# Query tails in 512-byte packets with quarter products, and other places for the choice products, three weight loads and the layout of the final choice

## The chip, the cores and the metric

The kernel runs on one core of one Trainium2 chip. The metric is the device time of one execution in microseconds (us), as the median over several runs. A core has five engines, each with its own in-order instruction stream: TensorE (PE, with its weight loads PEld), VectorE (DVE), ScalarE (ACT), GpSimd (POOL) and SyncE (SP). Here SP mostly issues transfers, and 16 DMA engines carry them out.

## The reference

Three layers, one behind the other. The first is a linear attention over 8 batches, 8 heads, 576 rows and a head width of 64; its output is normed per row and head. The rows then go through a mixture of 8 experts with one choice per row, and its output through a second mixture in which every expert takes exactly 576 rows.

```python
kv = np.einsum('bhsd,bhse->bhde', k, v)
out = np.einsum('bhsd,bhde->bhse', q, kv)
rms = np.sqrt(np.mean(out * out, axis=-1, keepdims=True) + 1e-06)
attn = out / rms * g_norm
...
logits = xn @ en.T / tau
expert_idx = np.argmax(logits, axis=1)
...
out[mask] = gate_w[mask, None] * (np.maximum(x[mask] @ w1[e], 0.0) @ w2[e])
...
flat = (x @ w_gate).flatten()
for idx in np.argsort(-flat):
    tok, e = int(idx) // E, int(idx) % E
    if assigned[tok] >= 0 or counts[e] >= cap:
        continue
    assigned[tok] = e
```

## The kernel before

**Attention.** The 8 batches go in 4 groups of 2 (`gi` 0 to 3). `kv(b)` multiplies k and v of a batch (line L295) and turns the result with the gate weights (L312). The queries go in 10 steps a group (`UNITS`): 8 steps of 4 heads by 256 rows, and 2 steps (`u == 4`) for the last 64 rows of each batch, the tail. `qa` transposes a step's queries on PE (L336) and copies them out on ACT (L337, `qT`); `qb` multiplies them with kv (L353, for the tail L359), and ACT and DVE carry the result out of PSUM (L368 or L370, L373, L375). `qa` runs two steps ahead of `qb`. The queries of 512 rows a batch come in by `load_main`, the tails by `load_tail`, where each packet is one row of one head, 64 floats or 256 bytes.

**Choice of the first expert.** When a group is done, `group_end` runs as a generator beside the next group's steps, a piece at each step: norms, the argmax, then `slots`, which counts the rows of each expert with two small matmuls against `trm` and `ones` (L477, L478, the "choice products"), and places each row by a matmul of one-hot rows (L517) into `table`. `WAITS` says how many steps `slots` holds back before the choice products and before L517. For the last group the generator runs beside the first expert's matmuls; `PEW` says how many us of those matmuls (after a plan of columns / 2400 us) PE issues between its pieces.

**First expert, early.** During the last group the first 320 rows of expert 0 are gathered; they are multiplied with their norms on DVE (`normed`, L654), transposed into tiles (`xtile`, L694), and split into a high half (ACT, L697) and a low half (DVE, L698). `XT0` names the step of each of the 3 tiles, its first entry also the step of the norms. Then `first0` streams layer 1 (L739, L740, L742) and `layer2_apart` (L810, L811, L808) through PE. Each weight is loaded raw (`wload`, on SP), cast on ACT (L567) and its low half taken on DVE (L573, partly put off into `LSUB`); three raw buffers go round. The remaining rows of expert 0 are gathered as soon as `tabi` (L1004) is there.

**Final choice.** After 8 rounds of bounds (`da_round`), `da_choice` writes the chosen expert of each row into `Pf` (L1193), and `table2` counts (L1250, L1251), scans (L1254) and places the rows (L1286). Matmuls of the last experts fill PE between the pieces.

In every engine the order is the order in which the program text calls; there is no scheduler.

## Time and profile before

| | |
|---|---|
| median of 3 runs | 1037.05 us (1033.49 to 1037.54) |
| profiled execution | 1037.28 us, of which the span of its instructions 1035.4 us |
| PE busy | 999.9 us, 97% of the span |
| DVE, ACT, POOL busy | 70%, 51%, 18% |
| DMA, 10 to 110 us | 16 engines busy throughout, 276 to 385 GB/s in stretches of 10 us |
| PE clock, mean | 0.995 of full |

The time is that of one execution from outside; the span runs from the first to the last instruction in the trace. The timeline gives for each row its start, its length, and in brackets how long the engine was idle before it and what ended that. A group of rows has one length for all of them. Matmuls in float32 are counted twice in these views (x16 for 8 instructions).

### The profile page before, as it was taken

The numbers are of one execution on the slowest core, as the hardware profiler recorded it, in microseconds if no ns is written. First come the engines' busy times: TensorE is split into PE (matmuls) and PEld (weight loads), VectorE is DVE, ScalarE is ACT, GpSimd is POOL, SyncE is SP. The second block draws the span as 40 slices with busy tenths as digits, with TensorE's granted clock in tenths as the row PEclk, the third lists the DMA queues.
The fourth block names the chain that finished last, engine by engine and source line by source line (L and its number), as shares of the span: only waits on it lengthen the run. The fifth ranks groups of instructions, "written<-read, shape, count | busy, mean of one in ns | idle before, by whom it ended". The sixth has DMA issues, their size and how long they took to land. (4 is left out here: it accounts for less than half of the span.)

```text
span 1035.4 us, 20479 instructions
## 1 busy us (share of the span) xinstructions
PE 999.9 (97%) x8177; PEld 920.5 (89%) x8177; DVE 729.5 (70%) x1513; ACT 528.0 (51%) x913; POOL 181.6 (18%) x310
## 2 busy tenths in 40 slices
PE   7888899999999999999999999999999999999998
PEld 6777799999999999999988889898989898989896
DVE  4466877569878878786876774859495858676760
ACT  2566836664545354444542323656555555656551
POOL 2000123101010201011001113131313132222211
PEclk9999999999999999999999999999999999999999
DMA  9999666544434344332402025342434242525211
GB/s 286 368 338 350 199 222 213 163 163 141 147 99 160 110 141 130 128 128 90 152 1 83 22 73 205 130 154 103 154 102 154 102 158 100 172 94 162 102 47 46
DMA packets 94679, 152.46 MB, mean 147 GB/s; under 512 B 11321, under 2 KB 52281, under 8 KB 94579
## 3 DMA queue, kind: packets, MB, share of 16 engines
q1 hardware_dynamic: 85539, 122.18, 35.4%
q0 software_dynamic: 9040, 28.93, 8.8%
q8 instruction: 65, 1.06, 0.4%
q14 instruction: 35, 0.29, 0.1%
HBM read 121.26 MB, written 29.82 MB: 146 GB/s over the span
## 5 line engine op out<-in xcount | busy, mean ns | idle before, releaser
L739 PE MATMUL mm<-xh,whi 128*128 128x256 f32 (+7 forms) x512 | 153.7, 300 | 0.9 <-ACT xh L697 0.5
L740 PE MATMUL mm<-xl,whi 128*128 128x256 f32 (+7 forms) x512 | 151.0, 295 | 0.3 <-issue 0.3
L742 PE MATMUL mm<-xh,wlo 128*128 128x256 f32 (+7 forms) x512 | 150.0, 295 | 0.0
L779 PE MATMUL mm<-hh,whi 128*128 128x256 f32 (+7 forms) x480 | 146.0, 304 | 0.0
L780 PE MATMUL mm<-hl,whi 128*128 128x256 f32 (+7 forms) x480 | 142.4, 297 | 0.0
L781 PE MATMUL mm<-hh,wlo 128*128 128x256 f32 (+7 forms) x480 | 142.1, 296 | 0.0
L573 DVE TENSOR_TENSOR wlo<-wraw,whi 128x1024 fp32r<-128x1024 f32 x71 | 86.5, 1223 | 32.1 <-ACT whi L567 31.0
L739 PEld LDWEIGHTS mm<-xh,whi 128*128 128x128 f32 x512 | 96.3, 188 | 2.4 <-ACT xh L697 0.7
L740 PEld LDWEIGHTS mm<-xl,whi 128*128 128x128 f32 x512 | 96.3, 188 | 0.5 <-issue 0.5
L742 PEld LDWEIGHTS mm<-xh,wlo 128*128 128x128 f32 x512 | 96.0, 188 | 0.0
L913 DVE SCALAR_TENSOR_TENSOR rc<-xg,big 128x512 bf16<-128x512 f32 x128 | 88.2, 689 | 8.6 <-ACT big L905 5.6
L779 PEld LDWEIGHTS mm<-hh,whi 128*128 128x128 f32 x480 | 91.3, 190 | 1.5 <-issue 0.5
L780 PEld LDWEIGHTS mm<-hl,whi 128*128 128x128 f32 x480 | 91.3, 190 | 0.0
L781 PEld LDWEIGHTS mm<-hh,wlo 128*128 128x128 f32 x480 | 90.8, 189 | 0.0
L791 ACT COPY yT<-mm 128x512 f32<-128x512 f32 (+7 forms) x29 | 18.5, 638 | 138.2 <-PE mm L781 138.2
L672 POOL DMA_INDIRECT xg<-xbuf,tabi x40 | 43.3, 1084 | 194.1 <-ACT sj L619 90.9
L567 ACT CAST whi<-wraw 128x1024 fp32r<-128x1024 f32 x71 | 73.9, 1043 | 1.2 <-DMA wraw<-in_moe_w 1.1
L748 ACT ACTIVATE hh<-mm 128x512 fp32r<-128x512 f32 (+7 forms) x56 | 36.8, 657 | 66.7 <-PE mm L742 66.0
L1943 DVE TENSOR_TENSOR wlo<-wraw,whi 128x1024 fp32r<-128x1024 f32 (+1 forms) x63 | 61.0, 988 | 11.6 <-ACT whi L1946 11.6
L2200 POOL DMA_INDIRECT out<-tm,ti x38 | 41.4, 1089 | 145.8 <-ACT tm L2198 126.3
L749 DVE SCALAR_TENSOR_TENSOR hl<-mm,hh 128x512 fp32r<-128x512 f32 (+7 forms) x56 | 42.7, 762 | 27.5 <-ACT hh L748 26.0
L2185 PE MATMUL mA<-whi,hx 128*128 128x512 f32 x136 | 56.9, 418 | 0.0
(402 smaller groups left out, 2607.7 us busy)
## 6 DMA issues: line engine op xcount, KB each, us to landing
wraw<-in_moe_w SPq DMA_DIRECT2D x127, 512.0 KB
kmain<-in_k SPq DMA_DIRECT2D x16, 576.0 KB
vmain<-in_v SPq DMA_DIRECT2D x16, 576.0 KB
xbuf<-xo SPq DMA_DIRECT2D x16, 528.0 KB
qmain<-in_q SPq DMA_DIRECT2D x16, 512.0 KB
ybuf<-yr SPq DMA_DIRECT2D x29, 260.0 KB
xg<-in_moe_w SPq DMA_DIRECT2D x16, 256.0 KB
xg<-in_moe_w_gate SPq DMA_DIRECT2D x8, 256.0 KB
```

What stands on the lines that cost most here:

```text
L567: nc.scalar.copy(hi, raw)
L573: eng.tensor_tensor(lo, raw, hi.bitcast(F32), op=OP.subtract)
L672: nc.gpsimd.indirect_dma_start(out=xg[:n, :wd], out_offset=None, in_=buf[:, :], in_offset=bass.IndirectOffsetOnAxis(ap=idx[:n, e * SC + t: ...
L739: nc.tensor.matmul(o, a, xh[:, kd, :N], start=(kd == 0), stop=False)
L740: nc.tensor.matmul(o, a, xl[:, kd, :N], start=False, stop=False)
L742: nc.tensor.matmul(o, b, xh[:, kd, :N], start=False, stop=(kd == KD - 1))
L779: nc.tensor.matmul(o, a, hh[:, kf, :N], start=(kf == 0), stop=False)
L780: nc.tensor.matmul(o, a, hl[:, kf, :N], start=False, stop=False)
L781: nc.tensor.matmul(o, b, hh[:, kf, :N], start=False, stop=(kf == KF - 1))
L913: V.scalar_tensor_tensor(junk, raws[i], 1.0, wgB[:, x], op0=OP.mult, op1=OP.mult, accum_out=w2g[:, i // KF, i % KF, x:x + 1])
L1943: V.tensor_tensor(l, x, h.bitcast(F32), op=OP.subtract)
L2185: nc.tensor.matmul(ps[:, x_, :], hh, a, start=(kf == 0), stop=False)
```

## The change

- `load_tail` brings the tail in packets of 2 rows of one head (512 bytes), in 4 transfers instead of 2 a group; partition 64 j + 32 hh + p holds rows 2p and 2p+1 of batch j for the heads of half hh.
- `qa` turns the whole tail at once (4 transposes and one copy of 512 columns, instead of twice 2 transposes and a copy of 256); `qb` forms the tail's products in quarters, 16 matmuls of 64 x 32 weights instead of 8 of 64 x 64 a step. Stores of the tail's rows and the row numbers (`tokf`) follow the new order, in 4 transfers instead of 2.
- The norms of expert 0's first tiles stay at step 5 (`NORM0`), the tiles move from steps 5, 6, 6 to 6, 6, 7. `WAITS` is per group: for group 2 the choice products go one step later, and L517 stays at its step.
- `PEW` changes, so that the last group's choice products and L517 are issued earlier between the first expert's matmuls. The low half of layer 1's last piece goes to `LSUB`, behind `table`, `tabi` and two low halves of weights.
- Three weight loads (8 to 10) leave `first0`'s put-off pieces on SP and are issued from ACT, one behind each of the tiles 3 to 5.
- `Pf` is stored by expert and then column, the order in which the matmuls and the sums of `table2` read it.

```diff
-PEW = (3.3, 6.2, 0.0, 0.4, 5.3)
+PEW = (3.3, 4.2, 2.0, 0.4, 4.1)
...
-XT0 = (5, 6, 6)
+NORM0 = 5
+
+XT0 = (6, 6, 7)
...
-WAITS = (1, 3)
+WAITS = ((1, 3), (1, 3), (2, 2), (0, 1))
...
-        t = mk(ap, [128, H, D], F32, nm + "tail", bufs=1)
+        t = mk(ap, [128, 4, 2, D], F32, "qtail", bufs=1)
         for j in range(2):
-            nc.sync.dma_start(t[64 * j:64 * j + 64], src(s, ((2 * gi + j) * H * S + 512) * D,
-                                                        [[D, 64], [S * D, H], [1, D]]))
+            for hh in range(2):
+                p = 64 * j + 32 * hh
+                nc.sync.dma_start(t[p:p + 32].rearrange("p h r d -> p h (r d)"),
+                                  src(q, ((2 * gi + j) * H * S + 4 * hh * S + 512) * D, [[2 * D, 32], [S * D, 4], [1, 2 * D]]))
...
+        if (u, hg) == (4, 1):
+            QT[gi, u, hg] = QT[gi, u, 0]
+            return
...
-            for h in range(2):
-                for s in range(2):
-                    for jj in range(2):
-                        nc.tensor.matmul(ov[64 * jj:64 * jj + 64, s, h],
-                                         qT[64 * s:64 * s + 64, h, 64 * jj:64 * jj + 64],
-                                         kvh(2 * gi + jj, 4 * hg + 2 * h + s)[64 * s:64 * s + 64, s], start=True, stop=True)
+            for h in range(4):
+                for jj in range(2):
+                    for r in range(2):
+                        p, c = 64 * jj + 32 * r, 64 * jj + 32 * hg
+                        nc.tensor.matmul(ov[p:p + 32, h % 2, h // 2], qT[64 * r:64 * r + 64, h, c:c + 32],
+                                         kvh(2 * gi + jj, 4 * hg + h)[64 * r:64 * r + 64, r], start=True, stop=True,
+                                         tile_position=(64 * r, p))
...
                 for j in range(2):
-                    b = 2 * gi + j
-                    nc.sync.dma_start(xbuf[b * S + 512:(b + 1) * S, :], x[64 * j:64 * j + 64, 0, :])
+                    for r in range(2):
+                        b, p = 2 * gi + j, 64 * j + 32 * r
+                        nc.sync.dma_start(xbuf[b * S + 512:(b + 1) * S, :].rearrange("(p r) d -> p r d", r=2)[:, r, :],
+                                          x[p:p + 32, 0, :])
...
+        def low(eng):
+            eng.scalar_tensor_tensor(hl, ps[:, :, :N], 0.0, hh.bitcast(F32), op0=OP.max, op1=OP.subtract)
+        if apart:
+            LSUB.append(low)
+        else:
+            low(V)
...
-            wcast(2 if f > 2 else 1, later=LSUB, ahead=3 if f else 4)
+            wcast(2 if f > 2 else 1, later=LSUB, ahead=4, load=(f == 0))
...
         xtiles(0, 0, 3 + i, 4 + i)
+        wload(RING + 1 + i, nc.scalar)
...
-    Pf = mk(mp, [128, NCOL, E], BF, "Pf")
+    Pf = mk(mp, [128, E, NCOL], BF, "Pf")
...
-        V.tensor_tensor(Pf, lm, m[:, :, None].to_broadcast([128, NCOL, E]), op=OP.is_ge)
+        V.tensor_tensor(Pf.rearrange("p e c -> p c e"), lm, m[:, :, None].to_broadcast([128, NCOL, E]), op=OP.is_ge)
...
-        Pe = Pf.rearrange("p c e -> p e c")
+        Pe = Pf
```

The order of PE's instructions around the first tail (group 0), before. `qtail` is the loaded tail, `kvx` the finished kv, `qT` the transposed queries; L359 are the tail's products, of which 2 of 8 are shown.

```order
L295 MATMUL mm<-kmain_87,vmain_88 64x64 x36
L336 MATMUL tp<-ident,qtail 128x128 x2
L353 MATMUL mm<-kvx_175,qT 128x144 x4
L312 MATMUL mm<-gex,kvn 128x72 x8
L336 MATMUL tp<-ident,qtail 128x128 x2
L353 MATMUL mm<-kvx_175,qT 128x144 x4
L295 MATMUL mm<-kmain_89,vmain_90 64x64 x36
L336 MATMUL tp<-ident,qmain 128x128 x4
L359 MATMUL mm<-kvx_174,qT 64x72
L359 MATMUL mm<-kvx_175,qT 64x72
```

The same place in the changed kernel, whose lines stand 3 to 16 further on (the products are L365, and 4 of 16 are shown).

```order
L298 MATMUL mm<-kmain_87,vmain_88 64x64 x36
L341 MATMUL tp<-ident,qtail 128x128 x4
L358 MATMUL mm<-kvx_177,qT 128x144 x4
L315 MATMUL mm<-gex,kvn 128x72 x8
L358 MATMUL mm<-kvx_177,qT 128x144 x4
L298 MATMUL mm<-kmain_89,vmain_90 64x64 x36
L341 MATMUL tp<-ident,qmain 128x128 x4
L365 MATMUL mm<-kvx_176,qT 32x72 x2
L365 MATMUL mm<-kvx_177,qT 32x72 x2
```

The four transposes stand together one step earlier, and each tail step has twice as many products of half the width.

The order on DVE in the last group, at steps 4 to 6, before. `s` are row sums of squares, `run` to `ue` the slot counts of group 2, `xg` and `kvx` the gathered rows of expert 0 under their norms (L654), `xl` the low half of their first tile (L698).

```order
L378 TENSOR_REDUCE s_1781<-sq 128x8 x2
L473 TENSOR_SCALAR run<-run 128x1
L482 SCALAR_TENSOR_TENSOR bs<-seg,sm 128x72
L484 TENSOR_TENSOR ue<-sm,run 128x72
L485 TENSOR_TENSOR ue<-ue,bs 128x72
L486 TENSOR_TENSOR run<-run,bs 128x8
L654 TENSOR_TENSOR xg_1822<-xg_1822 128x512
L654 TENSOR_TENSOR xg_1824<-xg_1824 128x512
L654 TENSOR_TENSOR kvx_174<-kvx_174 64x512
L378 TENSOR_REDUCE s_1781<-sq 128x8
L698 SCALAR_TENSOR_TENSOR xl_1962<-sm,gcol,xh_1961 128x4x128
L488 TENSOR_TENSOR ue<-ue,P 128x72
```

And in the changed kernel.

```order
L384 TENSOR_REDUCE s_1840<-sq 128x8 x2
L662 TENSOR_TENSOR xg_1881<-xg_1881 128x512
L662 TENSOR_TENSOR xg_1883<-xg_1883 128x512
L662 TENSOR_TENSOR kvx_176<-kvx_176 64x512
L384 TENSOR_REDUCE s_1840<-sq 128x8
L481 TENSOR_SCALAR run<-run 128x1
L490 SCALAR_TENSOR_TENSOR bs<-seg,sm 128x72
L492 TENSOR_TENSOR ue<-sm,run 128x72
L493 TENSOR_TENSOR ue<-ue,bs 128x72
L494 TENSOR_TENSOR run<-run,bs 128x8
L384 TENSOR_REDUCE s_1840<-sq 128x8
L706 SCALAR_TENSOR_TENSOR xl_2039<-sm,gcol,xh_2038 128x4x128 x2
```

The norms now stand ahead of the slot counts, and two tiles' low halves stand together behind them; the third tile's low half stands behind the ranks (`ue` to `sf`) as its second and third did.

The order on PE in `first0`, around the last group's choice products, before: L739 to L742 are layer 1's products in threes, and the rows behind L478 begin its last piece, in which they come in twos.

```order
L739 MATMUL mm<-xh_1961,whi 128x320
L740 MATMUL mm<-xl_1962,whi 128x320
L742 MATMUL mm<-xh_1961,wlo 128x320
L477 LDWEIGHTS trm
L477 MATMUL sm<-P,trm 128x72
L478 LDWEIGHTS ones
L478 MATMUL sm<-P,ones 128x72
L739 MATMUL mm<-xh_1961,whi 128x320
L740 MATMUL mm<-xl_1962,whi 128x320
L739 MATMUL mm<-xh_1961,whi 128x320
```

And in the changed kernel.

```order
L747 MATMUL mm<-xh_2038,whi 128x320
L748 MATMUL mm<-xl_2039,whi 128x320
L750 MATMUL mm<-xh_2038,wlo 128x320
L485 LDWEIGHTS trm
L485 MATMUL sm<-P,trm 128x72
L486 LDWEIGHTS ones
L486 MATMUL sm<-P,ones 128x72
L747 MATMUL mm<-xh_2038,whi 128x320
L748 MATMUL mm<-xl_2039,whi 128x320
L750 MATMUL mm<-xh_2038,wlo 128x320
```

The choice products now stand five threes earlier; L517 (not shown) stands five pairs of L810 and L811 earlier.

## Rows read from the trace of the kernel before

**Rows 1.** Head of the profile page.

```profile
span 1035.4 us, 20479 instructions
```

**Rows 2.** Stretches: us, busy PE, PEld, DVE, ACT, POOL; PE clock, DMA share, GB/s.

```profile
12.00:22.00 10.00, 7.37 (x192) 6.61 (x193) 4.79 (x21) 3.46 (x8) 0.00 (x0) 1.00 1.08 365
23.00:28.00 5.00, 3.35 (x88) 2.82 (x86) 1.38 (x2) 1.66 (x4) 0.00 (x0) 1.00 1.14 214
```

**Rows 3.** PE timeline: the longest wait for a load.

```profile
33.08 1.28 PE L295 MATMUL mm<-kmain,vmain 64*64 64x64 f32 x72 [2.28 <-DMA vmain<-in_v]
```

**Rows 4.** Transfers by line: the tails, with KB of one transfer.

```profile
qtail<-in_q SPq DMA_DIRECT2D x8, 128.0 KB
```

**Rows 5.** SP timeline: first tail load, and the weight loads 7 to 10.

```profile
16.97 3.29 SPq L142 DMA_DIRECT2D qtail<-in_q  x2
...
138.61 11.20 SPq L551 DMA_DIRECT2D wraw<-in_moe_w  x4
```

**Rows 6.** PE timeline: tail products, and rows beside them.

```profile
41.41 1.15 PE L353 MATMUL mm<-kvx,qT 128*128 128x144 f32 x8
...
47.86 0.48 PE L359 MATMUL mm<-kvx,qT 64*64 64x72 f32 x16
...
69.60 1.28 PE L295 MATMUL mm<-kmain,vmain 64*64 64x64 f32 x72
...
75.67 1.98 PE L312 MATMUL mm<-gex,kvn 64*128 64x72 f32 x16 [0.43 <-ACT lp L375]
...
82.70 1.28 PE L295 MATMUL mm<-kmain,vmain 64*64 64x64 f32 x72
...
103.70 1.11 PE L312 MATMUL mm<-gex,kvn 64*128 64x72 f32 x16 [1.71 <-ACT lp L375]
...
108.05 0.66 PE L336 MATMUL tp<-ident,qmain 128*128 128x128 f32 x4
```

**Rows 7.** DVE timeline: end of the last group, and its slot counts.

```profile
117.31 0.14 DVE L473 TENSOR_SCALAR run<-run 128x1 f32<-128x1 f32 x1
...
118.05 1.29 DVE L654 TENSOR_TENSOR xg<-xg 128x512 f32<-128x512 f32 x2
...
119.26 0.68 DVE L654 TENSOR_TENSOR kvx<-kvx 64x512 f32<-64x512 f32 x1
...
123.11 1.13 DVE L698 SCALAR_TENSOR_TENSOR xl<-sm,gcol,xh 128x512 fp32r<-128x512 f32 x2
...
136.63 0.30 DVE L482 TENSOR_TENSOR_SCAN bs<-seg,sm 128x72 f32<-128x72 f32 x1 [1.95 <-PE sm L478]
```

**Rows 8.** ACT timeline: wait for the counts, and third tile of the late rows.

```profile
117.49 0.20 ACT L474 COPY run<-run 128x8 f32<-128x8 f32 x1 [0.68 <-DVE run L473]
...
157.29 0.58 ACT L697 ACTIVATE xh<-tp,gcol 128x384 fp32r<-128x384 f32 x1 [1.66 <-PE tp L694]
```

**Rows 9.** PE timeline: first expert.

```profile
125.23 0.31 PE L740 MATMUL mm<-xl,whi 128*128 128x320 f32 x1
...
125.67 0.31 PE L740 MATMUL mm<-xl,whi 128*128 128x320 f32 x1
...
140.86 0.39 PE L810 MATMUL mm<-hh,whi 128*128 128x320 f32 x1 [0.75 <-DVE hl L749]
```

**Rows 10.** PE timeline: products of the final choice.

```profile
598.16 0.72 PE L1250 MATMUL mm<-Pf,ones 128*128 128x320 bf16 x1 [0.45 <-DVE Pf L1193]
...
599.38 0.30 PE L1252 MATMUL mm<-sl,ones 1*128 1x320 bf16 x1
```

**Rows 11.** DVE timeline: scan and masking of the final choice.

```profile
599.72 0.82 DVE L1254 TENSOR_TENSOR_SCAN rA<-seg,mm 128x320 f32<-128x320 f32 x1 [0.31 <-PE mm L1252]
...
601.36 0.74 DVE L1260 TENSOR_TENSOR rA<-rA,Pf 128x320 f32<-128x320 f32 x1
```

**Rows 12.** Two stretches, columns as in rows 2.

```profile
75.50:82.00 6.50, 6.33 (x48) 5.73 (x49) 1.76 (x3) 3.69 (x12) 0.00 (x0) 0.51 1.05 402
557.00:560.00 3.00, 3.00 (x17) 2.88 (x16) 2.48 (x7) 0.00 (x0) 0.87 (x1) 0.50 0.53 173
```

More of the change, by code (lines that the diff above doesn't have):

```diff
@@ L136, in fused_kernel, with load_tail @@
     LD = {}
-    def load_tail(gi, nm):
-        s = {"k": k, "v": v, "q": q}[nm]
-        t = mk(ap, [128, H, D], F32, nm + "tail", bufs=1)
+    def load_tail(gi):
+        t = mk(ap, [128, 4, 2, D], F32, "qtail", bufs=1)
         for j in range(2):
-            nc.sync.dma_start(t[64 * j:64 * j + 64], src(s, ((2 * gi + j) * H * S + 512) * D,
-                                                        [[D, 64], [S * D, H], [1, D]]))
-        LD[nm, "t", gi] = t
+            for hh in range(2):
+                p = 64 * j + 32 * hh
+                nc.sync.dma_start(t[p:p + 32].rearrange("p h r d -> p h (r d)"),
+                                  src(q, ((2 * gi + j) * H * S + 4 * hh * S + 512) * D, [[2 * D, 32], [S * D, 4], [1, 2 * D]]))
+        LD["q", "t", gi] = t
     def load_main(b, nm, hg):
@@ L222, in fused_kernel @@
     load_main(1, "q", 1)
-    load_tail(0, "q")
+    load_tail(0)
     load_kv(4)
@@ L329, in qa @@
         qT = mk(ap, [128, 4, 128], F32, "qT", bufs=3)
-        n = 4 if u < 4 else 2
-        for h in range(n):
+        for h in range(4):
             if u < 4:
@@ L334, in qa @@
             else:
-                a = LD["q", "t", gi][:, 4 * hg + 2 * h:4 * hg + 2 * h + 2, :]
+                a = LD["q", "t", gi][:, h]
             nc.tensor.transpose(pq[:, h, :], a.rearrange("p r d -> p (r d)"), ident)
-        nc.scalar.copy(qT[:, :n], pq[:, :n])
+        nc.scalar.copy(qT, pq)
         QT[gi, u, hg] = qT
@@ L346, in qb @@
         j, rr = divmod(u, 2)
-        qT = QT.pop((gi, u, hg))
+        qT = QT[gi, u, hg]
         po = mk(psum, [128, 2, 512], F32, "mm")
@@ L355, in qb @@
             ov = po[:, :, :2 * KW].rearrange("p a (c w) -> p a c w", w=KW)
-            for h in range(2):
-                for s in range(2):
-                    for jj in range(2):
-                        nc.tensor.matmul(ov[64 * jj:64 * jj + 64, s, h],
-                                         qT[64 * s:64 * s + 64, h, 64 * jj:64 * jj + 64],
-                                         kvh(2 * gi + jj, 4 * hg + 2 * h + s)[64 * s:64 * s + 64, s], start=True, stop=True)
+            for h in range(4):
+                for jj in range(2):
[4 more added lines that the diff above has]
+                                         tile_position=(64 * r, p))
         o3 = po[:, :, :n // 2 * KW].rearrange("p a (c w) -> p a c w", w=KW)
@@ L467, in slots @@
         def slots():
-            for i in range(0 if last else WAITS[0]):
+            for i in range(WAITS[gi][0]):
                 yield
@@ L512, in slots @@
                     [128, TG, NCOL // 2, 2]), op=OP.mult)
-            for i in range(1 if last else WAITS[1]):
+            for i in range(WAITS[gi][1]):
                 yield
@@ L570, in wcast, with rest @@
             up = WS["cast"] + ahead
-            def rest(eng, lo=lo, raw=raw, hi=hi, up=up):
+            def rest(eng, lo=lo, raw=raw, hi=hi, up=up, load=load):
                 eng.tensor_tensor(lo, raw, hi.bitcast(F32), op=OP.subtract)
@@ L706, in xtile @@
                 gate_in(e, t, p + n, xg)
-    GQ = []
+    GQ, LSUB = [], []
     def gates_in():
@@ L748, in layer1_g @@
         nc.scalar.activation(hh, ps[:, :, :N], AF.Relu)
-        V.scalar_tensor_tensor(hl, ps[:, :, :N], 0.0, hh.bitcast(F32), op0=OP.max, op1=OP.subtract)
+        def low(eng):
[4 more added lines that the diff above has]
+            low(V)
     tk = con([128, 2], I32, "tk")
@@ L970, in fused_kernel @@
         for j in range(2):
-            nc.gpsimd.iota(tokf[64 * j:64 * j + 64, gi, 8:9], pattern=[[0, 1]], base=(b0 + j) * S + 512,
-                           channel_multiplier=1, allow_small_or_imprecise_dtypes=True)
+            for r in range(2):
+                p = 64 * j + 32 * r
+                nc.gpsimd.iota(tokf[p:p + 32, gi, 8:9], pattern=[[0, 1]], base=(b0 + j) * S + 512 + r,
+                               channel_multiplier=2, allow_small_or_imprecise_dtypes=True)
     def split64(o, i, n):
@@ L1019, in fused_kernel @@
         if i == 9 and gi + 1 < NG:
-            load_tail(gi + 1, "q")
-        if gi == NG - 1 and i == XT0[0]:
+            load_tail(gi + 1)
+        if gi == NG - 1 and i == NORM0:
             for t in range(3):
@@ L1052, in fused_kernel @@
     MP[True] = mo0.enter_context(tc.tile_pool(name="moe0", bufs=1))
-    LSUB = []
     wload(RING - 1)
@@ L1685, in one_by_one @@
             V.tensor_tensor(Mv, Mv, ec[:, None, :].to_broadcast([128, NCOL, E]), op=OP.add)
-        V.tensor_copy(Pf.rearrange("p c e -> p (c e)"), A)
+        V.tensor_copy(Pf.rearrange("p e c -> p c e"), A.rearrange("p (c e) -> p c e", e=E))
         table2()
```

## The prediction, made before the change was run

> **What bounds the kernel now.** I read the head of the page first: the span is 1035.4 us [rows 1] and the profiled execution took 1037.28, so 1.9 us lie outside the span. The sum below is made against 1037.28; the median of the three runs, 1037.05, is 0.2 lower. Next I read the stretches by engine over the first 175 us, since nearly all of the change lies there, then the timelines of PE, DVE, ACT and SP around each edit, and last PE's and DVE's rows at the final choice. Outside these places PE is busy almost without a gap and no instruction differs, so every gain or loss has to show up as time that PE does not lose, or loses anew, at one of them.
>
> Four places matter. (1) Up to about 40 us the kernel runs at the pace of its loads. At 12 to 22 us the DMA engines are busy throughout (share 1.08) and move 365 GB/s; at 23 to 28 us they are just as busy and move 214 [rows 2]. PE feels it: at 33.08 its product of k and v had waited 2.28 us for a load [rows 3], the longest such wait; past 40 us there is none, the loads are ahead of PE. (2) From 45 to about 100 us PE sets the pace. (3) From 100 to 126 us ACT and DVE are loaded as heavily as PE, and a change of order on one of them moves the others. (4) From 125 us on PE is again the bound, with single waits that can be counted.
>
> **Tail loads.** A group's tail is 2 transfers of 128 KB [rows 4], 1024 packets of 256 bytes. SP issues the first at 16.97 [rows 5], behind 9 us of queued loads, and the dip at 23 to 28 is the only one in these 40 us, so I put it down to the tail. What the engines fell short of there is (365 - 214) x 5 / 365 = 2.1 us of full-rate time. The tail's own 262 KB take 0.7 us at full rate, so it cost 2.8 us of the engines. With half as many packets of twice the size the cost is between 2.8 (if only bytes counted, no gain) and 0.7 (if the dip vanishes, a gain of 2.1). I take cost by packet: half, 1.4, a gain of 1.4 us. It lies on the path because the loads for which PE waits at 33.08 were issued behind the tail [rows 3, 5], and 1.4 is less than the 2.28 of that wait. The three later tails meet loads that are ahead of PE: 0.
>
> The packet rule can be set against this. The Trainium skill, "DMA: Bandwidth & Descriptors", Specifications, gives 512 bytes as the smallest transfer for line rate. By that rule the whole dip goes, 2.1 instead of 1.4, and the sum would be 0.7 lower; the dip at 256 bytes agrees, and no run here shows 512.
>
> SP gets 4 issues for 2. The first two took 3.29 us [rows 5], as long as other issues among the backlog; SP here waits for the DMA engines and not they for SP, so I put the extra issues at 0. Their cover is the queue that keeps the engines busy; without it two more issues cost up to another 3.29. The stores of the tails also double. The last group's are not covered by loads, but the gather of the late rows waits for the choice (L517, `tabi`), which is later than they are.
>
> **Quarter products.** A tail step is 8 matmuls of 72 columns in 0.48 us; k by v is 36 of 64 columns in 1.28 [rows 6]. One more small matmul costs about (1.28 - 0.48) / 28 = 0.029 us, the rest is start-up. Eight more are 0.23 us a step; twice the whole row, 0.48, is the upper bound, and 36 matmuls in 1.28, so 16 in 0.57, the lower one: 0.1. Of the 8 tail steps, two in the last group and the first ones of groups 1 and 2 are followed by waits of PE on ACT that take it in (0.43 ahead of 75.67, 1.71 ahead of 103.70) [rows 6]; without these waits they would cost the same 0.23 each. Four steps count, 4 x 0.23 = +0.9 us (0.4 to 1.9). Four transposes and one copy of 512 columns for twice two and 256 is the same work in one piece: 0.
>
> **Order in the last group.** On DVE the three norms move ahead of L473. In before L473 runs at 117.31 and the norms at 118.05 to 119.86 [rows 7]; now the norms (1.81 us) and a row sum (0.6) come first, and L473 falls at about 119.7. ACT's second copy of `run` waits for it; it waited 0.68 us [rows 8] and will wait about 2, with the tail's copy, the next evacuation and the tiles behind it. But ACT has by then done the evacuation of step 5 (1.5 us) which stood behind this wait before. So ACT comes out level, at the tail's copy near 120.0. DVE does not: the first two tiles' low halves now wait for ACT until about 122.3, the ranks follow, and the third tile's low half, done at 124.2 before [rows 7], ends near 126.1. PE's first product with a low half, at 125.23 [rows 9], needs it: +0.9 us, with bounds of 0 and 1.5.
>
> In `first0` the opposite happens. DVE idled 1.95 us for the choice products [rows 7] and then had the low half of layer 1's third piece late, for which PE waited 0.75 us at 140.86 [rows 9]. The choice products now come five threes of 0.44 us [rows 9], 2.2 us, earlier. Even with the 0.9 from above they no longer leave DVE idle for long, and the third low half should be done more than 1 us ahead of PE: -0.75 (bounds 0 and -1). The last piece's low half goes behind `table`, `tabi` and two weight halves, but PE needs it only 7 us into the next layer: 0. What is late next there is the third tile of the late rows, for which PE stands briefly either way.
>
> **Weight loads.** Loads 7 to 10 held SP for 11.2 us from 138.61 [rows 5], mostly waiting for free buffers, and nothing urgent was behind them. Now 8 to 10 leave from ACT some 5 us later. Three issues now stand on ACT among the tile copies. One cost SP 1.6 us in the backlog of the first tail, or 2.8 in the mean of the four with their waits for buffers [rows 5]; neither backlog nor such a wait is left here, so both are upper ends. ACT idled 1.66 us ahead of the third tile at 157.29 [rows 8], which covers an issue. The first of these weights is cast some 4 us later. 0, with an upper bound of +1.
>
> **Final choice.** L1250 and L1251 read `Pf` with a stride and take 1.22 us together, from 598.16 to 599.38 [rows 10]. Read in order they should take about as long as L1252 each, 0.25. PE gains 0.7, but the scan that follows finds DVE busy until 599.4, so it moves only by its 0.31 wait, and the masking that reads `Pf` (0.74) falls to the 0.49 of other float32 rows of that size, -0.25 [rows 11]. PE waits for that chain at its next product, so the gain is the chain's: -0.56 (0 if writing `Pf` with a stride costs it, -0.9 at most).
>
> **Sum.** -1.4 + 0.9 + 0.9 - 0.75 + 0 - 0.56 = -0.9, so 1037.28 - 0.9 = 1036.4 us. With all lower bounds it is 1033.7, with all upper ones 1041.7.
>
> **Rivals.** First, the clock. PE was granted half its clock (1.2 for 2.4 GHz) at about 75.5 to 82 and at 557 to 560 [rows 12], the first behind a low stretch of PE. From 75.67 to 82.70 it did what took it from 103.70 to 108.05 at full clock [rows 6]: 7.0 less 4.35 is 2.7 us. The second cost about half of its 3 us, 1.4. The change shifts PE's instructions ahead of 75 us, and so may take the first away, or both: 1036.4 less 2.7 is 1033.7, less 4.1 is 1032.3. That one of the three runs took 1033.49 without any change speaks for it; that the others and the profile did not, against. This case decides "faster" only with both gone and a little more from the other terms.
>
> Second, a dip that vanishes: -2.1 for the tail load and 1035.7. This is what the page's packet rule would make of it.
>
> Third, on the other side, quarter products that do not overlap. Four full products (L353) of 144 columns take 1.15 us [rows 6], 0.29 each, so 72 columns alone on the array 0.14; if the pieces run one after the other at that pace, a step is 16 x 0.14 = 2.3 us instead of 0.48, and four steps cost +7.3: 1042.8. From +0.45 a step (twice my figure) the change is slower than before. The 0.029 us in [rows 6] is for pieces of 64 by 64 and speaks against it.
>
> Fourth, one more half-clock stretch where the new order leaves PE idle, at 118 to 126 us: +2.7 by the first one's price, 1039.1, slower than before by 2 us. For it: PE's idle time there grows to about 3.5 us; against: before had nearly as much and kept its clock.
>
> **Chances and range.** Forecast 0.45 (own range 1034.8 to 1038.0); clock restored 0.31; dip gone 0.10; further half-clock stretch 0.08; products without overlap 0.06. The three runs differ by 0.4%, so 0.5% (5.2 us) is about what can be told from no change: under 1031.9 is faster, over 1042.2 slower. Faster takes the lower half of the clock case, with some of the other terms at their lower bounds: 0.18. Slower is the third rival and mishaps of the fourth: 0.07. The range leaves out the lowest tenth and the highest: 1031.4 to 1039.4.
>
> **What would show it.** Right, if 23 to 28 us moves clearly more than 214 GB/s and PE's wait at 33 us shrinks to about 1; if a tail step takes near 0.7 us; if the first L748 starts about 0.9 us behind its L747 partner for want of `xl`; if the 0.75 us wait for `hl` is gone; if the two products of `Pf` take 0.5 us together. Wrong, if the load wait stays, if a tail step takes over 1 us, or if the clock's half stretches move: they weigh more than every term above.

## The result, and the profile after

The changed kernel took 1041.64 us in the median of 9 runs (1038.53 to 1047.42); the kernel before, beside it, 1033.49 to 1040.95 in 9 runs. The ratio is 1.0052, 95% interval 1.0033 to 1.0072: 5.4 us slower by that ratio (4.6 between the medians), above the range. The profiled execution took 1038.98 us, near the fastest of the nine and only 1.7 us above the one of before (1037.28), so no more than that can be looked for in this pair of profiles.

The page and the granted clock (windows: us, busy time by engine, clock, DMA share, GB/s) of the changed kernel. The queue `q8 instruction` brings program code, in packets of 16 KB (66 packets, 1.08 MB):

```profile
span 1037.2 us, 20756 instructions
...
q8 instruction: 66, 1.08, 0.4%
```

```profile
23.00:28.00 5.00, 2.29 (x76) 1.85 (x76) 1.38 (x2) 0.93 (x3) 0.00 (x0) 0.92 1.10 280
27.20:30.60 3.40, 3.40 (x30) 3.03 (x22) 0.00 (x0) 0.96 (x2) 0.00 (x0) 0.50 1.05 352
54.50:57.90 3.40, 3.40 (x65) 3.12 (x68) 1.50 (x4) 1.80 (x4) 0.00 (x0) 0.50 1.08 378
600.60:604.00 3.40, 3.40 (x18) 3.40 (x17) 3.12 (x11) 0.00 (x0) 0.00 (x0) 0.50 0.00 0
```

The span is 1.8 us longer than in [rows 1]. The dip at 23 to 28 us is 280 GB/s for 214 [rows 2]. The stretches at half clock (1.2 for 2.4 GHz) of [rows 12] are gone; three others stand at 27, 54 and 600 us, each right behind a long stand of PE (a time in which it does nothing), as PE's timeline of the changed kernel shows (the bracket is the wait ahead of the row and what ended it):

```profile
25.47 0.68 PE L298 MATMUL mm<-kmain,vmain 64*64 64x64 f32 x29 [2.25 <-DMA vmain<-in_v]
...
49.51 0.70 PE L365 MATMUL mm<-kvx,qT 64*32 64x72 f32 x32
50.14 0.44 PE L315 MATMUL mm<-gex,kvn 64*128 64x72 f32 x3
53.00 1.00 PE L315 MATMUL mm<-gex,kvn 64*128 64x72 f32 x13 [2.42 <-issue]
...
123.66 0.41 PE L747 MATMUL mm<-xh,whi 128*128 128x320 f32 x1 [0.40 <-ACT lp L381]
124.73 0.41 PE L748 MATMUL mm<-xl,whi 128*128 128x320 f32 x1 [0.66 <-DVE xl L706]
...
141.68 0.42 PE L824 MATMUL mm<-hh,whi 128*128 128x320 f32 x1 [0.55 <-ACT whi L575]
...
146.23 0.39 PE L824 MATMUL mm<-hh,whi 128*128 128x320 f32 x1 [1.54 <-DVE hl L759]
...
599.09 0.30 PE L1266 MATMUL mm<-Pf,ones 128*128 128x320 bf16 x1 [1.47 <-DVE Pf L1209]
599.23 0.30 PE L1267 MATMUL mm<-Pf,trm 128*128 128x320 bf16 x1
```

The same places in PE's timeline before, as far as [rows 3, 6, 9, 10] don't show them:

```profile
24.30 0.68 PE L295 MATMUL mm<-kmain,vmain 64*64 64x64 f32 x29 [1.08 <-DMA vmain<-in_v]
...
49.38 1.11 PE L312 MATMUL mm<-gex,kvn 64*128 64x72 f32 x16
...
52.39 1.50 PE L295 MATMUL mm<-kmain,vmain 64*64 64x64 f32 x72 [0.33 <-ACT kvx L317]
...
59.02 0.80 PE L295 MATMUL mm<-kmain,vmain 64*64 64x64 f32 x36 [1.42 <-issue]
...
66.17 0.58 PE L295 MATMUL mm<-kmain,vmain 64*64 64x64 f32 x24 [0.92 <-issue]
...
73.88 0.51 PE L353 MATMUL mm<-kvx,qT 128*128 128x144 f32 x2 [1.89 <-issue]
...
124.97 0.42 PE L739 MATMUL mm<-xh,whi 128*128 128x320 f32 x1 [0.16 <-ACT lp L375]
```

Four things are to be seen in this pair of profiles. The load wait moved from 33 to 25 us: 2.28 us there [rows 3] are gone, and 1.08 have become 2.25. Behind the first group's tails PE now stands 2.42 us inside the products of L315, for nothing that the view names ("issue"); before, these ran in one piece, and stands of the same name came later, at 59, 66 and 74 us. In `first0` the 0.75 us wait [rows 9] has become 0.55 and 1.54. And `Pf` comes 1.47 us late instead of 0.45 [rows 10].

DVE's timeline tells the last two. First `first0`, then the final choice, of the changed kernel:

```profile
142.61 0.24 DVE L529 TENSOR_TENSOR table<-table,sm 128x80 f32<-128x80 f32 x1 [2.55 <-PE sm L525]
142.88 0.20 DVE L1020 SCALAR_TENSOR_TENSOR tabi<-table 128x38 int32<-128x38 f32 x1
143.00 2.35 DVE L581 TENSOR_TENSOR wlo<-wraw,whi 128x1024 fp32r<-128x1024 f32 x2
145.27 0.82 DVE L759 SCALAR_TENSOR_TENSOR hl<-mm,hh 128x640 fp32r<-128x640 f32 x1
...
597.52 1.52 DVE L1209 TENSOR_TENSOR Pf<-rA,rm 128x320 bf16<-128x320 f32 x1
...
601.79 0.49 DVE L1276 TENSOR_TENSOR rA<-rA,Pf 128x320 f32<-128x320 f32 x1
```

The last piece's low half began 4.6 us after its `hh` was done (at 140.69 on ACT), and it reads that piece's PSUM tile. PSUM has two such tiles (`psum`, bufs 2), and layer 2 takes the second one for its columns `dp` 1: the wait stands ahead of the 13th pair of products, the first of `dp` 1, not at `kf` 6. The write of `Pf` with a stride of 40 elements took 1.52 us; before, in order, 0.49.

### The profile page after: what moved, and what is told of

It reads as the page before. It is cut to its first block, busy times and chain, and to the rows that moved or that the text cites. A ratio compares the mean times of both kernels' runs of the same rounds, so it can differ in the third digit from the quotient of the medians.

```text
span 1037.2 us, 20756 instructions
## 1 busy us (share of the span) xinstructions
PE 1000.3 (96%) x8305; PEld 922.0 (89%) x8305; DVE 729.8 (70%) x1513; ACT 527.1 (51%) x909; POOL 182.1 (18%) x318
## 3 DMA queue, kind: packets, MB, share of 16 engines
q8 instruction: 66, 1.08, 0.4%
## 5 line engine op out<-in xcount | busy, mean ns | idle before, releaser
L747 PE MATMUL mm<-xh,whi 128*128 128x256 f32 (+7 forms) x512 | 153.7, 300 | 1.2 <-ACT xh L705 0.5
L748 PE MATMUL mm<-xl,whi 128*128 128x256 f32 (+7 forms) x512 | 151.1, 295 | 0.9 <-DVE xl L706 0.9
L747 PEld LDWEIGHTS mm<-xh,whi 128*128 128x128 f32 x512 | 96.3, 188 | 2.9 <-DVE hl L759 0.8
L748 PEld LDWEIGHTS mm<-xl,whi 128*128 128x128 f32 x512 | 96.3, 188 | 1.4 <-DVE xl L706 1.4
```

What stands on the lines that cost most here:

```text
L747: nc.tensor.matmul(o, a, xh[:, kd, :N], start=(kd == 0), stop=False)
L748: nc.tensor.matmul(o, a, xl[:, kd, :N], start=False, stop=False)
```

## The experiments

Each ran beside the kernel before on the same chip; ratios are to that, with the 95% interval behind them. An amount in us is worked out from the ratio where nothing else is said.

**1. The parts.** Four kernels, of which the first three are the kernel before with a part of the diff, and the fourth takes one edit back:

```diff
# e1_tails_only:  + load_tail, qa, qb, the tails' stores and tokf
# e2_pf_only:     + the five lines on Pf
# e3_order_only:  + PEW, NORM0, XT0, WAITS, LSUB/low, wload on nc.scalar
# e4_low_at_once, against the changed kernel:
-        if apart:
-            LSUB.append(low)
-        else:
-            low(V)
+        low(V)
```

> The kernel before with the tails alone changed (512-byte loads and stores, quarter products, the new token order). Theory A (the loss sits at two places behind 140 us, where low halves and the final choice were moved): within 0.2% of the kernel before, 1036 to 1038 us, and the load wait of 2.28 us at 33 us is at most about 1. Theory B (the shifted attention part, with its smaller matmuls, is granted half clock more often): 3 to 5 us slower than before, near the changed kernel's 1041.6, and a mean clock near 0.990 instead of 0.995.

> The kernel before with only the layout of Pf changed. Theory A: the write of Pf with a stride takes 1.5 us instead of 0.49 and PE waits 1.4 to 1.5 us for it instead of 0.45; the two products take 0.37 us instead of 1.22, so the direct effect is within 0.3 us of nothing, and a stretch of half clock behind the wait can add 1.4: ratio 1.000 to 1.002. Theory B: the same within 0.1% of before, no half-clock stretch at 600 us. My forecast on record for this part was -0.56 us.

> The kernel before with the new order in the last group, the choice products moved, the low half put off and three weight loads from ACT, but with the old tails and the old Pf. Theory A: 1 to 3 us slower than before (ratio 1.001 to 1.003), with a wait of PE for hl of about 1.5 us near 146 us. Theory B: within 0.1% of the kernel before.

> The changed kernel with the low half of the last piece taken at once, as before, not put off behind the weights' low halves. Theory A: the wait of 1.54 us at 146 us goes or falls below 0.4, and the kernel is 1.2 to 1.6 us faster than the changed one, 1.003 to 1.004 of the kernel before; up to 3 us faster if a half-clock stretch often stands behind that wait. Theory B: the wait goes, but the time falls by no more than that 1.5 us, and the mean clock stays near 0.989.

Measured: tails alone 1.0019 (1.0001 to 1.0037), `Pf` alone 0.9993 (0.9976 to 1.001), order alone 1.0018 (1.0002 to 1.0034), low half at once 1.0118 (1.0092 to 1.0144). The order run has the wait of the changed kernel, in its PE timeline:

```profile
149.36 0.39 PE L818 MATMUL mm<-hh,whi 128*128 128x320 f32 x1 [1.54 <-DVE hl L753]
```

So theory A holds for the order, and B is not refuted: the tails, which were to cost nothing, cost something. `Pf` alone showed the same 1.52 us write, a wait of 1.48 us and products of 0.30 us, and no loss. The fourth run was expected to gain 1.5 us and lost 7. Its wait for `hl` is gone, but the timelines of PE, ACT and SP show a new one:

```profile
166.80 0.61 PE L747 MATMUL mm<-xh,whi 128*128 128x288 f32 x1 [4.69 <-ACT xh L705]
...
165.75 0.37 ACTq L559 DMA_DIRECT2D wraw<-in_moe_w  x1
166.17 0.58 ACT L705 ACTIVATE xh<-tp,gcol 128x384 fp32r<-128x384 f32 x1 [5.42 <-DMA ybuf<-yr]
...
158.04 5.33 SPq L1128 DMA_DIRECT2D ybuf<-yr  x8
```

ACT issues its second weight load only after the landing of a zero store of SP, and the third tile's copy stands behind it. In the changed kernel these stores left at 151.43 and the load at 156.63 without a wait. Why a load on ACT's queue waits for a store on SP's is not shown by a run. A second thing of this run stands in its times: its mean clock was the lowest of all (0.9835, before beside it 0.9916).

**2. The loads on ACT, the low half, and when the tail is loaded.**

```diff
# e5_loads_on_sp, against the changed kernel:
-            wcast(2 if f > 2 else 1, later=LSUB, ahead=4, load=(f == 0))
+            wcast(2 if f > 2 else 1, later=LSUB, ahead=3 if f else 4)
...
-        wload(RING + 1 + i, nc.scalar)
# e6_low_and_loads: e5 and low(V) at once;  e7_changed_again: no edit
# e8_tail_later, against e1:
-    load_tail(0)
     load_kv(4)
+    load_tail(0)
```

> The changed kernel with the three weight loads back on SP's queue, everything else as changed. Theory C (in most executions ACT stands ahead of one of these loads, as it did for 5.42 us in the run before this one where the low half was taken at once, and the tile copies behind it make PE wait; the changed kernel's own profile just missed it): 2 to 4 us faster than the changed kernel, ratio to before 1.001 to 1.003. Theory D (the loads on ACT cost the changed kernel nothing; the wait comes only where the low half is early): the same as the changed kernel, ratio 1.004 to 1.006.

> The changed kernel with the loads back on SP and the last piece's low half taken at once. Theory C: both waits are gone, from the first layer-2 product to the second expert 17.1 to 17.7 us as in the kernel before (17.06) instead of 19.15, ratio to before 1.000 to 1.002. Theory D: the loads were never the matter and the low half's gain comes on its own: 1.5 us faster than the changed kernel, ratio 1.003 to 1.004; and if something else than the load made ACT stand, the 4.7 us wait of PE for xh is here again, ratio over 1.009.

> The changed kernel itself once more, for a second profile and more times beside the others of this call. Theory C: the new profile shows ACT standing over 1 us ahead of a weight load at 154 to 160 us and PE waiting for xh behind it. Theory D: it shows the 1.5 us wait for hl again and no such wait; the time then differs from the first profile's only by the stretches at half clock. Both: ratio 1.004 to 1.007 to before, mean clock 0.988 to 0.990.

> The kernel of the first run of the last call (tails alone changed) with the first tail issued behind the loads of k and v of the fifth batch and not ahead of them. Theory E (the tail's packets went ahead of a load of v that PE waited for at 25 us, and the wait brought a half-clock stretch behind it): the wait at 25 us falls from 2.16 to about 1 us, no wait for a load over 1 us at 33, no half-clock stretch at 27 us, and the kernel is 1 to 2 us faster than with the tails alone, ratio to before 0.999 to 1.001. Rival F (the tails cost what they cost at the products and the fetch of the longer program): the wait moves or goes, but the ratio stays at 1.002.

Measured: 1.0061 (1.0041 to 1.0082) with the loads on SP, 1.0042 (1.002 to 1.0064) with the low half at once as well, 1.0054 (1.0034 to 1.0074) for the changed kernel again, 1.0039 (1.0022 to 1.0055) for the later tail. Theory C fell: the loads on ACT cost the changed kernel nothing, and its second profile has the waits of the first (0.56 and 1.54) and none for ACT. With the loads on SP the low half is worth 1.0061 less 1.0042, 2 us, which the two intervals leave open; the traces are plainer: the wait of 1.54 us for `hl` is in all four profiles in which the low half is put off (the changed kernel's two, the order alone, the loads on SP), and in none of the four with the new order in which it comes at once. The second expert starts in the run with both taken back 17.4 us after the first product of layer 2 (140.40 to 157.76), as before (140.86 to 157.92: 17.1) and not 19.15 as in the changed kernel. Theory E fell too, by the time: 1.0039 where 0.999 to 1.001 was expected. Its profile has no load wait at 25 or 33 us, but neither has the second profile of the changed kernel, whose loads were not moved.

**3. What the tails cost, and the order without the low half.**

```diff
# e9_quarters_only, against the kernel before:
-  nc.tensor.matmul(ov[64 * jj:64 * jj + 64, s, h], qT[64 * s:64 * s + 64, h, 64 * jj:64 * jj + 64], ...)
+  for c in range(64 * jj, 64 * jj + 64, 32):
+      nc.tensor.matmul(ov[c:c + 32, s, h], qT[64 * s:64 * s + 64, h, c:c + 32], ..., tile_position=(64 * s, c))
# e10_quarters_x4: e1 with each quarter product issued four times
# e11_tail_twice, against the kernel before:
+  for to in [<a raw weight buffer>, t] if gi == 0 else [t]:   # both loaded
# e12_order_plain: e3 without LSUB/low and without wload on nc.scalar
```

> The kernel before with each of the tail's 64 by 64 products cut into two of 64 by 32, loads and stores as before. Both theories: a tail step takes 0.70 us instead of 0.48. Theory K (only the four steps without a wait behind them count, as forecast): +0.9 us, ratio 1.0009. Theory L (all eight count): +1.8 us, ratio 1.0017. The two are too near each other for the times alone; the next run has to tell them apart.

> The kernel with the tails alone changed (first run of the first call), with each quarter product issued four times, the same values again. By the 0.0275 us of one piece a tail step grows from 0.70 to about 2.0 us. Theory K (four of the eight steps count): 5 to 6 us slower than with the tails alone, ratio to before 1.007 to 1.009. Theory L (all eight): 10 to 11 us slower, ratio 1.012 to 1.014. Rival: small products lower the clock; then the mean clock falls by more than 0.003 and the ratio is above 1.014.

> The kernel before with the first group's tail loaded twice, the first time into a buffer that nobody reads: 1024 more packets of 256 bytes ahead of the same loads, 2.8 us of the DMA engines by the forecast's working. Theory G (these engines set the pace there, so the forecast's -1.4 for 512-byte packets was a real gain): the wait at 33 us grows to about 5 us and everything behind it is 2 to 2.8 us later, ratio 1.002 to 1.003. Theory H (PE is held by something else by 50 us and the gain is given back there): the wait grows but the first product of k and v of the fifth batch (52.39 us) moves by less than 0.7 us, ratio 1.000 to 1.001.

> The kernel before with the new numbers for the order alone (slots of the choice, tiles one step later, waits of the choice), without the put-off low half and without the loads on ACT. Theory M (what the order run lost of the time, ratio 1.0018, was the low half's 2.1 us): ratio 0.999 to 1.001, no wait for hl over 0.3 us behind 139 us. Theory N (the order itself costs): ratio 1.0015 to 1.002 as in that run.

Measured: 1.0035 (1.0016 to 1.0054), 1.0267 (1.024 to 1.0295), 1.0018 (0.9997 to 1.004), 0.9999 (0.9979 to 1.0019). For the order itself no cost is seen (theory M); with the low half put off and the loads moved it was 1.0018, and the intervals of the two overlap. The surprise is the first. Its PE timeline:

```profile
51.10 0.48 PE L360 MATMUL mm<-kvx,qT 64*32 64x72 f32 x32
...
54.75 1.00 PE L312 MATMUL mm<-gex,kvn 64*128 64x72 f32 x13 [2.64 <-issue]
```

A tail step there takes 0.48 us, as long as with half as many pieces (four pieces that follow each other lie side by side there, which I take for the reason; no run shows it); the loads and stores are the old ones, and still it is 3.6 us slower. What it shares with the changed kernel is the number of PE's instructions and the stand behind the first tails. In the run with four times as many pieces a step takes 4.88 us, not 2.0, since the repeats run one after the other (128 rows, 0.038 us each):

```profile
82.19 4.88 PE L364 MATMUL mm<-kvx,qT 64*32 64x72 f32 x128
```

Of 8 x (4.88 - 0.48) = 35.2 us, 27.7 arrived in the time, as much as six of eight steps. That does not decide between K and L: K's waits, 0.43 and 1.71 us long [rows 6], can hide 0.22 us a step but not 4.4, and the numbers of both rested on the wrong step. Its mean clock was the highest of all kernels run (0.9957, before 0.9908 beside it), so small products don't lower the clock by themselves. Loading the tail twice is inconclusive by its time: the interval holds both theories.

**4. The number of instructions.**

```diff
# e13_halves_twice, against the kernel before: the 64 by 64 product issued twice
+  for _ in range(2):
# e14_quarters_late: as e9, but 32 wide only if gi > 1, else 64 wide
# e15_quarters_shift (on e9) and e16_before_shift (on the kernel before):
-            nc.tensor.transpose(pw[:, 128 * (i % 4):128 * (i % 4) + 128], ident, ident)
-    warm(44)
+            nc.tensor.matmul(pw[:64, 128 * (i % 4):128 * (i % 4) + 52], ident[:, :64], ident[:, :52], ...)
+    warm(108)
```

> The kernel before with each 64 by 64 product of the tails issued twice, the same values again: as many instructions of PE as with the quarter products, but no narrow pieces. Theory R (what costs is 256 more instructions in PE's stream where it is being fetched through loaded queues, and with them one more long stand of PE and its half-clock stretches): as slow as the run with quarters only, ratio 1.002 to 1.005, a wait named issue of 2.4 us or more behind the first tails at 53 us, mean clock about 0.002 lower than before's. Theory S (the narrow pieces themselves): ratio 1.000 to 1.001, mean clock as before's.

> The kernel before with quarter products in the tails of the third and fourth group only, as before in the first two. Theory R with its place at the first group's tails (the wait of 2.6 us at 53 to 55 us and the stretch behind it): ratio 0.999 to 1.001, and no wait named issue over 2 us at 52 to 56 us. If the cost lies in every group alike: ratio 1.0015 to 1.002.

> Quarter products in all tails, as in the run with quarters only, but PE's 44 warming transposes at the start are 108 short products, so that every later instruction lies 128 further on in PE's stream (half of one 16 KB fetch). Theory R1 (where the fetch boundaries fall decides): the wait of 2.64 us at 54.75 moves by 2 us or more or splits, and the ratio differs from the 1.0035 there by more than 0.0015. Theory R2 (the count alone decides): ratio 1.003 to 1.0045. Theory S: 1.003 to 1.004.

> The kernel before with the same 108 short products at the start for the 44 transposes, so that every fetch boundary of PE's stream moves by half of one fetch. Theory R1: the waits named issue move (1.42 us at 59.02 and 1.89 at 73.88 in the profile before), with them the half-clock stretch at 75.5, and the time changes by more than 0.15% either way. Theory R2: ratio 1.000 to 1.001 with 128 instructions more. Theory S: 0.999 to 1.001.

Measured: 1.0044 (1.0027 to 1.0061), 1.0008 (0.9991 to 1.0025), 1.0089 (1.0062 to 1.0117), 1.0075 (1.0053 to 1.0096). The shifts say little on boundaries by their times: the 108 short products were not short, PE reached its first product of k and v 6 to 7 us late, and in the traces this product stands 344 instructions later in PE's stream, not 128. The start without quarters:

```profile
1.53 15.42 PE L955 MATMUL sm<-ident 128*64 128x52 f32 x216 [1.53 <-DVE ident L182]
```

Against each other they give the quarter products' cost once more, 2.8 us between the medians (1045.69 and 1042.87) and 1.5 by the ratios; by the intervals it could also be nothing. The doubled 64 by 64 products, which are not narrow, stand at the same place as the quarters, in its PE timeline:

```profile
51.14 0.80 PE L360 MATMUL mm<-kvx,qT 64*64 64x72 f32 x32
...
54.58 1.00 PE L312 MATMUL mm<-gex,kvn 64*128 64x72 f32 x13 [2.27 <-issue]
```

They cost 4.6 us. Their longer steps (0.80 for 0.48, eight times) explain at most 2.6 of it; the lower end of the interval, 2.8, lies just above that. So theory S, narrow pieces, is out as the only cause, by a small margin, and R, the number of instructions, stands.

**5. The place, and what can be taken back.**

```diff
# e17_quarters_early: as e9, but 32 wide only if gi < 2, else 64 wide
# e18_mended, against the changed kernel: low(V) at once, wload on SP, the old Pf, and
-                for jj in range(2):
-                    for r in range(2):
+                for r in range(2):
+                    for jj in range(2):
```

> The kernel before with quarter products in the tails of the first two groups only, the counterpart of the run with the last two. Theory R (the cost comes from the instructions of PE added in the first half of the attention part, where the loads keep the DMA queues full): nearly all of the 3.4 us of the run with quarters only, ratio 1.0022 to 1.0035. If each group costs alike: 1.0015 to 1.002. If it lies in the last two after all: 1.000 to 1.001.

> The changed kernel with its two found losses taken back (low half at once, weight loads on SP), the old layout of Pf, and the quarter products of one row half next to each other. By the parts measured so far (tails 2.8 us, new order 0.4, low half 0, Pf 0, and 0 to 1.4 us back if the new sequence shortens a tail step from 0.70 towards 0.48): 1.8 to 3.2 us slower than before, ratio 1.0017 to 1.003, about 2 to 3 us faster than the changed kernel. Rival: the parts do not add up, and the ratio stays above 1.004 as in the run with the low half and the loads taken back.

Measured: 1.0036 (1.0016 to 1.0056) and 1.004 (1.0022 to 1.0058). As the ratios stand, the cost of the quarter products lies in the first two groups (1.0036, for 1.0008 with the last two); an equal share of some 1.0017 in either half lies in both intervals, though, and is not excluded. PE's timelines of the run with the early quarters, and of the one with the late ones:

```profile
50.95 0.48 PE L361 MATMUL mm<-kvx,qT 64*32 64x72 f32 x32
51.52 0.44 PE L312 MATMUL mm<-gex,kvn 64*128 64x72 f32 x3
54.38 1.00 PE L312 MATMUL mm<-gex,kvn 64*128 64x72 f32 x13 [2.42 <-issue]
```

```profile
50.79 0.48 PE L361 MATMUL mm<-kvx,qT 64*64 64x72 f32 x16
51.31 1.12 PE L312 MATMUL mm<-gex,kvn 64*128 64x72 f32 x16
```

The kernel with everything taken back that could be gained 1.3 us on the changed one in ratio (1.0040 for 1.0052 and 1.0054), less than hoped; the new sequence of pieces left a step at 0.70 us. It agrees with the tails (1.0019 and 1.0039) and the plain order (0.9999) within their intervals. No version was faster than the kernel before by more than its interval.

## Why the prediction was wrong

**The failed steps are two: "Quarter products" and "Order in the last group" in its part on `first0`. A third term, "Tail loads", was mis-sized.** By the parts that were run alone: the tails as a whole +2 to +4 us (1.0019, 1.0039) for -0.5 forecast (-1.4 + 0.9), the waits in `first0` +1.3 for -0.75, the order 0 for +0.9, `Pf` -0.7 (0.9993) for -0.56. That adds up to 2.6 to 4.6 us, of 5.4 measured (3.4 to 7.5 by the interval).

**Quarter products, +0.9 forecast.** The step's length was right (0.70 for 0.48). Wrong was to price the pieces by their time on the array alone, and at nothing as instructions that PE has to be sent: with no longer steps and the old loads they cost 3.6 us, the same in the first two groups alone (3.7 us), 0.8 in the last two; and products that are not narrow, but as many, 4.6. Whether it also counted too few steps is not shown.

What PE stands for inside L315 is its code. The 20 profiles have 116 stands named issue of 0.3 us or more between 10 and 115 us. Counted along PE's stream in the trace (matmul rows, weight loads and the few instructions of its sequencer), the instructions behind these stands lie whole multiples of 256 apart, to within one: numbers 705, 1217, 1473, 1729, 1985 and so on. And 256 instructions are one packet of the code queue: before, 16519 are in the trace and 65 packets; the quarters add 256 and one packet. Each of the 116 stands ended 0.9 to 1.9 us after such a packet had landed. In the changed kernel one ran from 50.53 to 51.62 us, and PE went on at 53.00 with number 1729; before, one ran from 56.64 to 57.73, and PE went on at 59.02 with number 1985. From 37 to 64 us these packets started 6.4 to 7.0 us apart before, so a packet of 256 instructions that PE works off in less leaves it standing. A matmul in float32 is two rows and two weight loads in that count, so 8 more in a tail step are 32 more instructions.

The stand of 2.3 to 2.7 us at number 1729 is in every profile with twice as many products in the first group's tails, and in none without; with four times as many it falls among the pieces (1.96 us), and with another start of PE's stream it is 1.38 us with the quarters and without. Up to there the loss can be seen: the fifth batch's k and v products start at 55.7 to 58.6 us in the eleven profiles with twice as many products in the first two groups' tails, and at 52.1 to 55.3 in the six without (56.42 and 52.39 in the profiles after and before).

**Where these 3 us lie in the end stays open.** By the first product of the expert the profiles no longer show them: it starts at 125.0 us on average in the eleven and at 125.8 in the six (123 to 128 in both). The stands for code don't hold them either: from 10 to 115 us they come to 6.2 us in the changed kernel and 5.8 before, 6.2 to 9.0 in the eleven (7.6 on average), 5.4 to 8.3 in the six (6.9). The stand at 53 us is new, those at 59 and 66 are gone. Over all executions, not only the profiled ones, the mean clock of nine kernels with twice as many products in the first two groups' tails was 0.0007 to 0.0044 below that of before beside them, on average 0.0023 (of two more, that with the low half at once was 0.0081 below, the shifted one 0.0015 above). Between executions of one kernel (least squares, a term for each kernel and chip) 0.001 of the clock goes with 0.5 us, so a third of the loss would go with the clock. For two thirds there is no row, and why the instructions cost in the whole what they cost is not shown.

**The low half in `first0`, -0.75 forecast; it cost 2.1 us of waits in place of 0.75, +1.3.** "PE needs it only 7 us into the next layer: 0" looked at the operand (`kf` 6 and 7) and not at the PSUM tile that the low half reads. That tile was wanted after 12 pairs, 3.5 us in. Runs with and without it differ by 2 us twice (1.0018 and 0.9999; 1.0061 and 1.0042), neither time clear of the intervals, and in the first pair the loads on ACT differ too. The other half of the step, that the 0.75 us wait goes, held, but a weight cast on ACT (0.55 us) was late next, also where the low half was at once.

**Tail loads, -1.4 forecast; a third of that in the engines' work, and no gain that the runs show.** From 23 to 28 us the changed kernel moved 280 GB/s for 214 [rows 2]. Over all profiles the step is smaller: eight that loaded the first tail once in packets of 256 bytes, with the old start of PE, moved 211 to 267 there (240 on average), eight with 512 bytes, issued at the same place, 265 to 289 (280). By the forecast's own working that is 40 x 5 / 365 = 0.5 us. The packets say the same: in that window one of 256 bytes took 34 ns of its DMA engine on average (739 packets before), one of 512 bytes 46 ns (354 after), so a pair of rows became a third cheaper, where the forecast took half. Nor was the wait at 33 us a mark of the old packets: of the first eight profiles two have it (2.28 and 2.27 us), two have 1.81 and 1.96 us at 25 us instead, as the changed kernel has 2.25, and four have neither. PE's waits for loads from 10 to 122 us come to 3.2 to 6.0 us in the first eight (6.0 before) and to 3.0 to 4.9 in the others (4.9 in the changed kernel). The profiles with 3.0 to 3.4 have one thing in common that no edit made: PE was at half clock for 10 us from 12 us on, in the changed kernel's second profile, for one, and not in its first. Among them is the run that loaded the tail twice; it moved only 185 GB/s in the dip, and its fifth batch still began at 54.92 us, between 54.67 and 55.25 of two kernels that loaded it once (plain order, `Pf` alone). With that start, at least, the tail's packets did not set PE's pace. By the rule of the Trainium skill ("DMA: Bandwidth & Descriptors", Specifications) that 512 bytes are the smallest transfer for line rate, read as the forecast read it, the dip would be gone; the 280 GB/s, for 365 in [rows 2], say that more than half of it stays.

**Order in the last group, +0.9 forecast.** L748 did wait for `xl` (0.66 us), but in this profile L747 started earlier, and the order by itself measured 0.9999 (0.9979 to 1.0019): 0.

**Weight loads, 0 forecast.** Right on average (1.0061 without, 1.0054 with them). The upper bound of +1 was too small: with the low half early, ACT stood 5.42 us.

**Final choice, -0.56 forecast.** The two products take 0.30 us each, as L1252 does in [rows 10] (the forecast read 0.25 there), and 0.44 together, since they overlap (0.5 forecast); the masking takes 0.49, as forecast. But the bound "0 if writing `Pf` with a stride costs it" was what came. The writer lost 1.03 us, PE's wait grew by as much, and the gains of 0.85 on PE and 0.25 on the chain about make up for it: 0.9993 (0.9976 to 1.001) in time.

**The rivals.** None was the mechanism of the loss. Products that don't overlap would have given a step of 2.3 us; it is 0.70. The clock's stretches did move, as feared. The fourth rival, a stretch at half clock where the new order leaves PE idle (chance 0.08), is not in the two profiles of the changed kernel, but in all six others with the new order a stretch of 3.4 or 6.8 us starts between 119 and 129 us, as in this window of the run with the loads on SP:

```profile
123.70:127.10 3.40, 2.90 (x11) 2.90 (x12) 3.33 (x10) 0.02 (x1) 0.00 (x0) 0.50 0.00 0
```

None of the twelve profiles with the old order has one there. So that rival was more likely than it was given, though it did not make the order slower in the mean: the run with the plain order has a stretch of 6.8 us there in its profile, and its ratio is 0.9999.

## What to carry to other kernels

A low-priority operation that is put off holds what it reads as well as what it writes: ask who wants the buffer next, not only who wants the result. Small matmuls are to be counted as instructions, not only by their time on the array, wherever the engine already stands for nothing that the view names: count along its stream and look at the code queue's packets to see whether it stands for code. Here 128 more rows of PE and as many weight loads cost over 3 us with steps no longer than before, most of it, as it seems, by the half in the first two groups. One pair of profiles is not enough to price a wait: the load wait at 33 us, on which a term rested, came and went between executions with the same loads. A layout that makes the reader's access straight makes the writer's crooked: price both, and see which of them PE waits for.

## What was not expected of the hardware

Thirty-two rows of 64 by 32 pieces took 0.48 us where four successive ones filled the array's columns from the same rows, 0.70 in the changed kernel's sequence, and 0.038 us each when the same piece was repeated. PE stood for its code at 116 places in 20 profiles, up to 2.9 us, while the load queues were full: 16 KB packets of code came 6.4 to 7.0 us apart. A bf16 write of 320 elements a partition took 1.52 us with a stride of 40 elements for 0.49 in order. The kernel with the busiest PE in the attention part had the highest mean clock (0.9957) though it was the one with the most small products.
